# Top-32 attention with two feed-forward layers on one core: v in ten chunks of 128 rows with a column of ones, and three products per chunk into the same 65 columns

## The chip, the core and the metric

The kernel runs on one core of a Trainium2 chip. The core has five engines that work side by side, each through its own instructions in order: TensorE (PE, matrix products; its weight loads are listed apart as PEld), VectorE (DVE), ScalarE (ACT), GpSimd (POOL) and SyncE (SP, which issues the transfers). They wait for each other by semaphores. PE writes its products to a small memory of its own, PSUM, in eight banks; the rest lies in SBUF. The metric is the time of one execution on the device, in microseconds (us), as the median of several runs.

## What is computed

Four batches of eight heads with 576 positions of 64 values each. Every row of the scores keeps its 32 largest entries, the softmax runs over those, and the result goes through two feed-forward layers of 512 x 2048 x 512.

```python
scores = scale * np.matmul(q, k.transpose(0, 1, 3, 2))
kth = np.partition(scores, -top_k, axis=-1)[..., -top_k:-top_k + 1]
scores = np.where(scores >= kth, scores, -1000000000.0)
attn = np.exp(scores - np.max(scores, axis=-1, keepdims=True))
attn = attn / (np.sum(attn, axis=-1, keepdims=True) + 1e-09)
attn_out = np.matmul(attn, v)
x = attn_out.transpose(0, 2, 1, 3).reshape(B * S, H * D)
h = x @ moe_w_in;   x = np.maximum(0.01 * h, h) @ moe_w_out
h = x @ moe2_w_in;  out = (h * (1.0 / (1.0 + np.exp(-h)))) @ moe2_w_out
```

## The kernel before

**Numbers in two halves.** Every fp32 operand of a product is kept as a sum of two fp16 numbers, hi and lo, after a scaling by a power of two. A product is then hi times hi, hi times lo and lo times hi, added up in PSUM. The power of two comes from a sum of squares: ACT squares a tile and adds up each row (`kvsq`, L606), PE sums over the rows with a matrix of ones (`sum`, L550), and three small DVE steps make the factor.

**Blocks and pairs.** The 2304 positions are 18 blocks of 128 rows. Sixteen blocks lie in one batch. Two *mixed* blocks (numbers 4 and 13, from zero) hold the last 64 positions of two batches, the one in rows 0 to 63 and the other in rows 64 to 127. A block has four *pairs* of heads, so there are 72 pairs, 64 pure and 8 mixed; pair 12 below is the thirteenth. For each pair:

- `S` (L748): PE multiplies q and k into 2 x 576 scores; ACT copies them to SBUF (L760).
- `chain`: fourteen DVE steps, MAX8 and MATCH_REPLACE8 by turns (L774 to L778), find the 32nd largest of each row.
- `cut` and `exp` (ACT, L800 and L809): what is below the cut goes to zero in the exponential. `exp` also sums the row (`accum_out`, a separate ACCUMULATOR read), into `rs`.
- `p_hi` (ACT, L824) and `p_lo` (POOL, L832) make the halves of the probabilities, and a transfer transposes them into `pT`, 18 chunks of 128 positions by 128 rows.
- `pv` (PE, L862): for each of the two heads and each batch of the block ten products. The 1152 positions of two heads lie in nine chunks of v, `[128, 9, 2, D]`: four full ones for each head, and a middle one, number 4, of which each head has 64 rows. For a full chunk p_hi is multiplied with v_hi and v_lo side by side (128 columns) and p_lo with v_hi (64 columns). For the middle one both contract 64 rows only.

After two pairs (half a block) DVE makes the reciprocals from `rs` (`norm`, L878 and L884), ACT copies the v_lo columns out of PSUM (`comb_a`, L897), DVE adds the others (`comb_b`, L902), and POOL multiplies by the reciprocals (`comb_c`, L909) into `xf`.

**Feed-forward.** Per block and layer there are four steps of twelve matmuls of 512 columns into `h` (L986; from `xT` in the first layer and `yT` in the second), the activation and split on ACT, DVE (L1004, second layer only) and POOL (L1020), a transposing transfer, and four steps of twelve matmuls into `acc` (L1039). That is 16 steps of twelve matmuls per block, 288 in all.

**Weights.** In the first quarter of the span the four weight matrices are loaded as int64 words, rebuilt as fp32 by ACT and DVE (L438, L475), squared on PE (L492) for their scale, and split into halves by ACT, POOL and DVE (L527 is DVE's share of the splits).

**What sets the order.** A planner (`Plan.run`) works out the order of all engines ahead of time. Every step has an engine, a duration that is written into the code (`pv`: 1.3 us per batch), what it reads and writes, and the buffers that it takes (`BUFS`: one tile for `S`, `pv`, `acc` and `hlk`, two for `h`, three for `g`, five for `v`). By these costs and two tables of delays and preferences (`LATE`, `BOOST`) it always picks the step that can begin first, and each engine then gets its instructions in that fixed order. A changed cost can therefore move any step.

**Where v's buffers bind.** v has five tiles and a batch needs four. At a mixed block, the second batch's v tiles take the tiles of the first batch, one by one, as their last `pv` is done. The conversion `kvhi` (L632) takes the tile, so it waits for that `pv`; the square, the sum and the scaling run ahead of it.

Of the kernel before, what the change touches and what calls it, by code (L numbers as in the profile page):

```python
# [279 lines left out]
def topk_attention_moe_moe2_kernel(  # L280
# [34 lines left out]
    junk = wp.tile([128, 9 * D], BF16, name="junk")  # L315
# [265 lines left out]
    def kv_ops(which, src, b, p):  # L581
# [29 lines left out]
        add("ACT", act_t(576) + 0.1, square, r=[rk], w=[("kvss", which, b, p)], name="kvsq" + tail)  # L611
# [16 lines left out]
        def hi():  # L628
            tile_of(dk, "hlk" if which == "k" else "v", [128, 9, 2, D], F16)
# [5 lines left out]
            new=[("hlk", dk), ("k", ("k", b, p))] if which == "k" else [("v", dk)], name="kvhi" + tail, seq="kvhi")  # L635
# [95 lines left out]
    def pair_ops(s):  # L731
# [51 lines left out]
        for h in range(2):  # L783
# [345 lines left out]
```

## Time and profile before

| what | value |
| --- | --- |
| median of 3 runs | 1118.65 us (1118.25 to 1121.33) |
| span of the profiled execution | 1120.1 us, its own time on the page |
| PE, busy | 987.2 us (88%) |
| DVE, busy | 898.8 us (80%) |
| ACT, busy | 845.0 us (75%) |
| POOL, busy | 650.5 us (58%) |
| `pv` on PE (L862), 1600 matmuls, busy | 112.6 us |
| both feed-forward layers on PE (L986, L1039), busy | 797.5 us |

Busy times of an engine are the union of its instructions. Matmuls are pipelined: one is listed with some 0.2 to 0.4 us, from its start to its modelled end, and the next begins long before that. The time that a group of matmuls costs PE is therefore read from its first start to the first start of the next group.

### The profile page before, as it was taken

How to read it: one execution, taken by the hardware profiler on the slowest of the kernel's cores; microseconds unless marked ns; L12 is line 12 of the kernel's file. 1: busy time of each engine (PE TensorE's matmuls, PEld its weight loads, DVE VectorE, ACT ScalarE, POOL GpSimd, SP SyncE). 2: the span in 40 equal slices, each digit the busy share in tenths (PEclk: the TensorE clock that was granted, in tenths of full speed). 3: DMA queues.
4: the chain of work that ended last, by engine and by line, in shares of the span. 5: the costliest groups of instructions: out<-in, count | busy, mean ns of one | idle time of the engine just before them, and what ended most of it. 6: DMA issues, size and time to landing. Idle time of an engine off the chain costs nothing.

```text
span 1120.1 us, 18054 instructions
## 1 busy us (share of the span) xinstructions
PE 987.2 (88%) x6024; PEld 494.9 (44%) x6024; DVE 898.8 (80%) x1853; ACT 845.0 (75%) x1415; POOL 650.5 (58%) x885
## 2 busy tenths in 40 slices
PE   2443664879999999999999999999999999999998
PEld 1222323344444544444444544445555444444443
DVE  5999878999948999999999999974999999720000
ACT  5999998989767888887897888774888786742322
POOL 1355664869565776666786676664576655542321
PEclk9655676989999999999999999999999999999999
DMA  7995876635876687675987885776567675653432
GB/s 221 313 312 156 229 212 186 145 76 105 155 145 109 120 163 132 122 137 111 182 159 134 147 146 114 131 134 135 105 132 130 123 122 97 117 101 70 69 70 57
DMA packets 458110, 157.44 MB, mean 141 GB/s; under 512 B 440864, under 2 KB 449056, under 8 KB 455968
## 3 DMA queue, kind: packets, MB, share of 16 engines
q1 hardware_dynamic: 458016, 156.29, 67.1%
q8 instruction: 47, 0.77, 0.3%
q14 instruction: 47, 0.39, 0.1%
HBM read 47.71 MB, written 4.72 MB: 47 GB/s over the span
## 4 chain that ended last, share of the span: by engine, by line
PE 46%; DVE 26%; ACT 11%; issue 6%; POOL 6%; DMA 4%; SPq 1%; ACTq 0%; POOLq 0%; DVEq 0%
PE acc L1039 19%; PE h L986 18%; DVE w L776 9%; DVE m L778 8%; PE pv L862 4%; PE S L748 3%; DVE w_all L475 2%; DVE m L774 2%; POOL ph L832 2%; DMA pT<-ph 2%; ACT sb L809 2%; ACT sb L800 1%; PE acc L492 1%; ACT ph L824 1%; DVE w_all L527 1%
## 5 line engine op out<-in xcount | busy, mean ns | idle before, releaser
L1039 PE MATMUL acc<-w_all,gT 128*128 128x512 f16 x1728 | 400.1, 382 | 15.9 <-POOL w_all L532 5.0
L778 DVE MAX8 m<-w 128x8 f32<-128x576 f32 x432 | 307.9, 746 | 0.0
L1020 POOL TENSOR_TENSOR hl<-g,hl 128x512 f16<-128x512 f32 x144 | 173.6, 1206 | 164.2 <-ACT hl L1013 157.6
L1039 PEld LDWEIGHTS <-gT 128*128 128x128 f16 x1728 | 166.1, 99 | 213.5 <-issue 19.8
L832 POOL TENSOR_TENSOR ph<-sb,ph 128x1152 f16<-128x1152 f32 x72 | 171.1, 2376 | 114.6 <-ACT ph L824 104.8
L986 PE MATMUL h<-w_all,xT 128*128 128x512 f16 x864 | 201.4, 385 | 16.5 <-DMA xT<-hlx 15.8
L776 DVE MATCH_REPLACE8 w<-m,w 128x576 f32<-128x576 f32 x288 | 211.9, 742 | 0.0
L986 PE MATMUL h<-w_all,yT 128*128 128x512 f16 x864 | 196.0, 379 | 1.7 <-DVE g L1004 1.7
L986 PEld LDWEIGHTS <-xT 128*128 128x128 f16 x864 | 84.3, 99 | 118.0 <-DMA xT<-hlx 16.7
L809 ACT ACTIVATE sb<-sb,nb,u 128x576 f32<-128x576 f32 x144 | 124.1, 862 | 16.0 <-POOL nb L788 10.7
L986 PEld LDWEIGHTS <-yT 128*128 128x128 f16 x864 | 83.8, 98 | 100.3 <-issue 2.3
L862 PE MATMUL pv<-v,pT 128*128 128x128 f16 (+3 forms) x1600 | 112.6, 214 | 14.6 <-DMA pT<-ph 14.6
L800 ACT ACTIVATE sb<-sb,m 128x576 f32<-128x576 f32 x144 | 108.5, 766 | 21.2 <-DVE m L778 20.9
L1004 DVE SCALAR_TENSOR_TENSOR g<-g,h 128x512 f32<-128x512 f32 x72 | 48.9, 680 | 93.5 <-ACT g L999 91.0
L774 DVE MAX8 m<-sb 128x8 f32<-128x576 f32 x144 | 101.9, 745 | 11.0 <-ACT sb L760 11.0
L862 PEld LDWEIGHTS <-pT 128*128 128x128 f16 (+3 forms) x1600 | 87.4, 103 | 52.2 <-DMA pT<-ph 16.8
L760 ACT ACTIVATE sb<-S 128x1152 f32<-128x1152 f32 x72 | 81.0, 1125 | 37.6 <-POOL ph L832 30.7
L748 PE MATMUL S<-k,qT 128*128 128x64 f16 (+3 forms) x640 | 90.1, 301 | 19.3 <-DMA qT<-hlx 9.3
L1013 ACT ACTIVATE hl<-g 128x512 f16<-128x512 f32 x144 | 89.9, 625 | 21.7 <-DVE g L1004 18.1
L776 DVE MATCH_REPLACE8 w<-m,sb 128x576 f32<-128x576 f32 x144 | 105.9, 742 | 0.0
L788 POOL TENSOR_SCALAR nb<-m,u 128x1 f32<-128x1 f32 x144 | 67.7, 473 | 53.2 <-DVE m L778 50.5
L824 ACT ACTIVATE ph<-sb 128x1152 f16<-128x1152 f32 x72 | 83.5, 1159 | 5.0 <-DMA pT<-ph 3.7
(96 smaller groups left out, 1024.1 us busy)
## 6 DMA issues: line engine op xcount, KB each, us to landing
w_all<-in_moe_w_in_dram SPq DMA_DIRECT2D x16, 1024.0 KB, 5.8
w_all<-in_moe_w_out_dram SPq DMA_DIRECT2D x14, 1024.0 KB, 6.0
raw<-in_k_dram SPq DMA_DIRECT2D x16, 256.0 KB, 3.1
rawq<-in_q_dram SPq DMA_DIRECT2D x32, 128.0 KB, 2.8
raw<-in_v_dram SPq DMA_DIRECT2D x16, 256.0 KB, 3.0
out_dram<-of SPq DMA_DIRECT2D x16, 256.0 KB, 2.4
gT<-hl SPq DMA_TRANSPOSE x144, 3.2
of<-in_moe_w_out_dram SPq DMA_DIRECT2D x8, 256.0 KB, 3.1
```

What stands on the lines that cost most here:

```text
L748: nc.tensor.matmul(out=t[p0:p1, o:o + k1 - k0], lhsT=lhs, rhs=kt[:, k0:k1], start=(x == 0), stop=(x == 1),)
L774: nc.vector.max(m[:, 0], T[sbk][:, h])
L776: nc.vector.match_replace(w, m[:, step // 2], T[sbk][:, h] if step == 1 else w, NEG)
L778: nc.vector.max(m[:, step // 2], w)
L800: nc.scalar.activation(out=x, in_=x, func=AF.Prelu, scale=-1.0, bias=T["m", s][:, h, 3, 7:8], alpha=2.0**-CUT)
L809: nc.scalar.activation(out=x, in_=x, func=AF.Exp, scale=T["u", blk, hf][:, 1, p % 2:p % 2 + 1], bias=T["nb", s][:, h:h + 1], accum_out=T[" ...
L824: nc.scalar.activation(out=T[phk][:, 0, x0 * S:x1 * S], in_=T[sbk][:, x0:x1].rearrange("p h k -> p (h k)"), func=AF.Copy)
L832: nc.gpsimd.tensor_tensor(out=T[phk][:, 1, x0 * S:x1 * S], in0=T[sbk][:, x0:x1].rearrange("p h k -> p (h k)"), in1=T[phk][:, 0, x0 * S:x1 ...
L862: nc.tensor.matmul(out=o[p0:p1, h, p % 2, 0:n], lhsT=l, rhs=r, start=(i == 0), stop=(i == len(mm) - 1))
L986: nc.tensor.matmul(out=t, lhsT=a[:, ai], rhs=w_rhs(layer, wi, kk, i), start=(n == 0), stop=(n == 3 * KDM - 1))
L1020: nc.gpsimd.tensor_tensor(out=n[:, 1], in0=T[gk], in1=n[:, 0], op=ALU.subtract)
L1039: nc.tensor.matmul(out=t, lhsT=g[:, ai], rhs=w_rhs2(layer, wi, 4 * i + j), start=(i == 0 and j == 0 and n == 0), stop=(i == NCH - 1 and j ...
```

## The change

- **v** becomes `[128, 10, 129]`: 64 columns hi, one column of ones, 64 columns lo. The middle chunk stands there twice, once for each head, with zeros in the rows of the other. Four POOL instructions per v tile (`vtail`) write the ones, the copy and the zeros.
- **pv**: for each of five chunks per head, p_hi and p_lo are multiplied with v_hi and the ones (65 columns), and p_hi with v_lo (64 columns), all into the same 65 columns, always over 128 rows. That is 15 instead of 10 matmuls per head and batch, 2400 instead of 1600. In a mixed block the loop over the batches is the inner one. The planner's cost goes from 1.3 us per batch to 0.87 us, and 1.02 us for a mixed pair.
- **Row sums and combining**: the 65th column is the row sum, so `exp` no longer sums. `norm` reads the sum from PSUM, and one DVE step (`comb`) multiplies the 64 columns by the reciprocals into `xf`; `comb_a` on ACT and `comb_c` on POOL are gone. The tile in PSUM takes one bank instead of two.
- **Squares**: `kvsq` writes its squares into the v tile (or the k tile `hlk`) that it takes for that, before, not at, the conversion. The other squares go to a tile `junk` in the freed PSUM bank.
- The scaled copy of the second layer's input takes a tile of `of` instead of one of `g`.

```diff
+    VW = 2 * D + 1
-    junk = wp.tile([128, 9 * D], BF16, name="junk")
+    junk = ps.tile([128, 512], F32, name="junk", tag="junk", bufs=1)
...
         def square():
             T["kvss", which, b, p] = st_tile(1, f"kvss{which}", 4)
+            tile_of(dk, "hlk" if which == "k" else "v", [128, 9, 2, D] if which == "k" else [128, 10, VW], F16)
             nc.scalar.activation(
-                out=junk[:, 0:9 * D], in_=T[rk].rearrange("p c d -> p (c d)"), func=AF.Square,
-                accum_out=T["kvss", which, b, p],
+                out=dst(0).bitcast(BF16), in_=T[rk], func=AF.Square, accum_out=T["kvss", which, b, p],
             )
...
+        if which == "v":
+            def tails():
+                t = T[dk]
+                nc.gpsimd.memset(t[:, 0:9, D:D + 1], 1.0)
+                nc.gpsimd.tensor_copy(t[ST:128, 9, :], t[ST:128, 4, :])
+                nc.gpsimd.memset(t[0:ST, 9, :], 0.0)
+                nc.gpsimd.memset(t[ST:128, 4, :], 0.0)
+
+            add("POOL", 1.0, tails, w=[dk], name="vtail" + tail)
...
-                    bias=T["nb", s][:, h:h + 1], accum_out=T["rs", blk][:, c:c + 1],
+                    bias=T["nb", s][:, h:h + 1],
...
-                tile_of(pvk, "pv", [128, 2, 4, 128], F32)
+                tile_of(pvk, "pv", [128, 2, 2, D + 1], F32)
...
+                o = T[pvk][:, p % 2, h]
+                mm = []
+                for c, vc in [(5 * h + c, 5 * h + c) for c in range(4)] + [(4, 9 if h else 4)]:
+                    mm += [(c, vc, 0, D + 1), (9 + c, vc, 0, D + 1), (c, vc, D + 1, VW)]
+                for i, (c, vc, d0, d1) in enumerate(mm):
+                    for p0, p1, b, _ in blocks[blk]:
                         nc.tensor.matmul(
-                            out=o[p0:p1, h, p % 2, 0:n], lhsT=l, rhs=r, start=(i == 0), stop=(i == len(mm) - 1)
+                            out=o[p0:p1, 0:d1 - d0], lhsT=pT[:, c, p0:p1], rhs=T["v", b, p][:, vc, d0:d1],
+                            start=(i == 0), stop=(i == len(mm) - 1),
                         )
-        add("PE", 1.3 * len(bs), pv, r=[pTk] + [("v", b, p) for b in bs], w=[pvk],
+        add("PE", 0.87 + 0.15 * (len(bs) - 1), pv, r=[pTk] + [("v", b, p) for b in bs], w=[pvk],
...
-                    in0=T["rs", blk][p0:p1, 4 * hf:4 * hf + 4].rearrange("p (j h) -> p j h", h=2), scalar=1e-9,
+                    in0=T[pvk][p0:p1, :, :, D], scalar=1e-9,
...
+            nc.vector.tensor_tensor(
+                out=T[xk][:, 256 * hf:256 * hf + 256].rearrange("p (j h d) -> p j h d", h=2, d=D), in0=T[pvk][:, :, :, 0:D],
+                in1=T["rec", blk, hf].rearrange("p (j h o) -> p j h o", h=2, o=1).to_broadcast([128, 2, 2, D]), op=ALU.mult,
+            )
...
-                t = tile_of(yk, "g", [128, DM], F32)
+                t = tile_of(yk, "of", [128, DM], F32)
```

**On PE, the start of one pair's pv.** Before, after the sum for a v tile, each weight load of a chunk of `pT` is followed by a matmul of 128 or of 64 columns:

```order
L550 MATMUL h<-kvssv,ones 128x1
L862 LDWEIGHTS pT
L862 MATMUL pv<-v,pT 128x128
L862 LDWEIGHTS pT
L862 MATMUL pv<-v,pT 128x64
```

In the changed kernel, at the start of the same pair's pv (behind the squares of a weight matrix):

```order
L493 MATMUL acc<-w_all 128x128
L866 LDWEIGHTS pT
L866 MATMUL pv<-v,pT 128x65
L866 LDWEIGHTS pT
L866 MATMUL pv<-v,pT 128x65
L866 LDWEIGHTS pT
L866 MATMUL pv<-v,pT 128x64
```

A chunk has three narrow products where it had a wide and a narrow one.

**On DVE, at pair 12 of the attention.** Before, between the MAX and MATCH_REPLACE steps of pair 12 (`m_2041`), stand a split of the last weight matrix (L527) and gating steps of the second layer (L1004):

```order
L776 MATCH_REPLACE w<-m_2041,w 128x576 x2
L1004 SCALAR_TENSOR_TENSOR g<-g,h 128x512
L778 MAX m_2041<-w 128x8 x2
L527 SCALAR_TENSOR_TENSOR w_all<-w_all,ws_2035 128x1024
L1004 SCALAR_TENSOR_TENSOR g<-g,h 128x512
```

In the changed kernel pair 12 runs without a step of another kind, and among those of pair 13 (`m_2153`) stand the trace of the last weight matrix (L503), its scale (`ws_2261`), the two steps of `norm` and the new `comb` (L898), and the first split (L528):

```order
L503 SCALAR_TENSOR_TENSOR junk,wtot<-acc,ident 128x128
L788 MAX m_2153<-w 128x8
L883 SCALAR_TENSOR_TENSOR den<-pv,sv_75 128x4
L889 RECIPROCAL rec<-den 128x4
L356 TENSOR_SCALAR fx<-h 128x1
L357 TENSOR_SCALAR ws_2261<-fx 128x1
L358 TENSOR_SCALAR ws_2261<-fx 128x1
L898 TENSOR_TENSOR xf<-pv,rec 128x256
L786 MATCH_REPLACE w<-m_2153,w 128x576 x2
L528 SCALAR_TENSOR_TENSOR w_all<-w_all,ws_2261 128x1024
```

The splits of the last weight matrix have moved behind a later pair, and with them the layer steps that need it.

**On ACT, behind the first pv of mixed block 4.** Before, the conversion of v (L632) waits for PE, with the conversion of k and the first layer's square behind it:

```order
L824 ACTIVATE ph<-sb 128x1152
L685 ACTIVATE rawq<-rawq,qs 128x256
L632 ACTIVATE v<-raw 128x9x64
L632 ACTIVATE hlk<-raw,sk_72 128x9x64
L924 ACTIVATE junk,xss<-acc 128x512
```

In the changed kernel the square into the v tile (L608) waits there, and its scaling (L628) and conversion (L635) follow some steps later:

```order
L833 ACTIVATE ph<-sb 128x1152
L608 ACTIVATE v,kvssv<-raw 128x9x64
L991 ACTIVATE g<-h,u_2284 128x512
L930 ACTIVATE of<-acc,ys 128x512
L682 ACTIVATE junk,qss<-rawq 128x256
L1005 ACTIVATE hl<-g 128x512
```

What now begins behind that pv is the whole preparation of the v tile, not its last steps.

## Rows read from the trace of the kernel before

**Rows 1.** Page: busy us (share, instructions); busy tenths in 40 slices.

```profile
PE 987.2 (88%) x6024; PEld 494.9 (44%) x6024; DVE 898.8 (80%) x1853; ACT 845.0 (75%) x1415; POOL 650.5 (58%) x885
PE   2443664879999999999999999999999999999998
...
DVE  5999878999948999999999999974999999720000
```

**Rows 2.** Stretches: length, busy us (instructions) of each engine, PEclk, DMA share, GB/s.

```profile
0.00:100.00 100.00, 36.33 (x243) 24.26 (x244) 83.73 (x166) 81.58 (x114) 35.06 (x48) 0.70 0.91 270
100.00:200.00 100.00, 57.41 (x331) 30.84 (x330) 86.38 (x146) 90.26 (x133) 61.87 (x63) 0.65 0.67 188
...
278.25:322.70 44.45, 40.71 (x260) 19.84 (x258) 40.88 (x89) 35.68 (x64) 27.84 (x38) 0.96 0.82 147
322.70:998.46 675.76, 670.04 (x4227) 332.84 (x4227) 602.55 (x1294) 532.20 (x933) 431.95 (x623) 1.00 0.70 130
998.46:1120.10 121.64, 117.98 (x561) 53.67 (x559) 11.12 (x16) 36.40 (x60) 32.32 (x39) 1.00 0.35 68
```

**Rows 3.** PE's timeline near 600 us: start, us to the last end, instructions.

```profile
601.89 1.14 PE L748 MATMUL S<-k,qT 128*128 128x512 f16 x8
602.87 2.75 PE L986 MATMUL h<-w_all,xT 128*128 128x512 f16 x12
605.46 2.75 PE L1039 MATMUL acc<-w_all,gT 128*128 128x512 f16 x12
608.05 1.33 PE L862 MATMUL pv<-v,pT 128*128 128x128 f16 x20
609.31 2.76 PE L986 MATMUL h<-w_all,xT 128*128 128x512 f16 x12
```

**Rows 4.** A stretch inside that pv, L862 alone: length, PE, PEld busy.

```profile
608.39:608.48 0.09, 0.09 (x4) 0.01 (x1) 1.00 0.06 24
```

**Rows 5.** PE's timeline at mixed blocks: scores and the next, pv and the next.

```profile
336.20 1.20 PE L748 MATMUL S<-k,qT 128*64 128x512 f16 x16
337.33 1.47 PE L986 MATMUL h<-w_all,xT 128*128 128x512 f16 x6
...
759.81 2.73 PE L862 MATMUL pv<-v,pT 128*64 128x128 f16 x40
762.47 0.82 PE L1039 MATMUL acc<-w_all,gT 128*128 128x512 f16 x3
```

**Rows 6.** Pair 12's pv; then L986 alone and L1039 alone up to it.

```profile
278.25 1.32 PE L862 MATMUL pv<-v,pT 128*128 128x128 f16 x20
...
0.00:278.25 278.25, 47.82 (x192) 19.48 (x192) 0.75 0.73 197
...
0.00:278.25 278.25, 33.49 (x132) 12.82 (x132) 0.75 0.73 197
```

**Rows 7.** Groups by line and form: count, busy us, mean ns, idle before it.

```profile
L862 PEld LDWEIGHTS <-pT 128*128 128x128 f16 x1024 | 55.8, 103 | 34.5 <-DMA pT<-ph 16.8 <-issue 0.8
L862 PEld LDWEIGHTS <-pT 128*64 128x64 f16 x256 | 12.9, 111 | 4.6 <-issue 3.0
L527 DVE SCALAR_TENSOR_TENSOR w_all<-w_all,ws 128x1024 f16<-128x1024 f32 x15 | 20.7, 1383 | 0.0
L1004 DVE SCALAR_TENSOR_TENSOR g<-g,h 128x512 f32<-128x512 f32 x72 | 48.9, 680 | 93.5 <-ACT g L999 91.0 <-POOL hl L1020 1.9
L809 ACT ACTIVATION_READ_ACCUMULATOR sb<-sb,nb,u 128x1 f32 x144 | 27.1, 188 | 0.0
L606 ACT ACTIVATE junk<-raw 128x576 bf16<-128x576 f32 x32 | 21.5, 673 | 4.2 <-DMA raw<-in_k_dram 2.9 <-DMA raw<-in_v_dram 1.3
L643 POOL TENSOR_TENSOR v<-raw,v 128x576 f16<-128x576 f32 x12 | 15.3, 1279 | 3.4 <-ACT v L632 3.4
L356 POOL TENSOR_SCALAR xs<-fx 128x1 int32<-128x1 int32 x18 | 3.4, 190 | 1.5
```

**Rows 8.** Waits: who waited for whom, us in total, times, longest.

```profile
ACT v L632 <- PE pv L862: 4.2, 3, 2.3
```

More of the change, by code (lines that the diff above doesn't have):

```diff
@@ L605, in square @@
             T["kvss", which, b, p] = st_tile(1, f"kvss{which}", 4)
+            tile_of(dk, "hlk" if which == "k" else "v", [128, 9, 2, D] if which == "k" else [128, 10, VW], F16)
             nc.scalar.activation(
[L607 to L611 removed]
+                out=dst(0).bitcast(BF16), in_=T[rk], func=AF.Square, accum_out=T["kvss", which, b, p],
+            )
+        add("ACT", act_t(576) + 0.1, square, r=[rk], w=[dk, ("kvss", which, b, p)],
+            new=[("hlk" if which == "k" else "v", dk)], name="kvsq" + tail)
         sum_op(("kvss", which, b, p))
@@ L619, in dst @@
         def dst(x):
+            if which == "v":
+                return T[dk][:, 0:9, (D + 1) * x:(D + 1) * x + D]
             return T[dk][:, :, x, :]
@@ L634, in kv_ops @@
         add("ACT", act_t(576, 1), hi, r=[rk, sn], w=[dk],
-            new=[("hlk", dk), ("k", ("k", b, p))] if which == "k" else [("v", dk)], name="kvhi" + tail, seq="kvhi")
+            new=[("k", ("k", b, p))] if which == "k" else [], name="kvhi" + tail, seq="kvhi")
         def lo():
@@ L886, in comb_ops, with comb @@
         add("DVE", 0.16 + 0.17 * len(bs), norm,
-            r=[("rs", NP * blk + 2 * hf + j, h) for j in range(2) for h in range(2)]
-            + [("s", "v", b, 2 * hf + j) for b in bs for j in range(2)],
+            r=[pvk] + [("s", "v", b, 2 * hf + j) for b in bs for j in range(2)],
             w=[("rec", blk, hf)], name="norm" + tail)
-        def half():
-            return T[xk][:, 256 * hf:256 * hf + 256].rearrange("p (j h d) -> p j h d", h=2, d=D)
-        def comb_a():
+        def comb():
             if hf == 0:
                 tile_of(xk, "xf", [128, DM], F32)
-            nc.scalar.activation(out=half(), in_=T[pvk][:, :, 0:2, D:2 * D].rearrange("p h j d -> p j h d"), func=AF.Copy)
-        add("ACT", act_t(256), comb_a, r=[pvk], w=[(xk, hf)], new=[("xf", xk)] if hf == 0 else [], name="comb_a" + tail, seq="comb_a")
-        def comb_b():
-            nc.vector.tensor_tensor(out=half(), in0=T[pvk][:, :, 0:2, 0:D].rearrange("p h j d -> p j h d"), in1=half(), op=ALU.add)
-        add("DVE", 0.35, comb_b, r=[pvk], w=[(xk, hf)], name="comb_b" + tail)
-        def comb_c():
-            r = T["rec", blk, hf].rearrange("p (h o) -> p h o", o=1).to_broadcast([128, 4, D])
-            dst = T[xk][:, 256 * hf:256 * hf + 256].rearrange("p (h d) -> p h d", d=D)
-            nc.gpsimd.tensor_tensor(out=dst, in0=dst, in1=r, op=ALU.mult)
-        add("POOL", 0.65, comb_c, r=[("rec", blk, hf)], w=[(xk, hf)], name="comb_c" + tail)
+            nc.vector.tensor_tensor(
+                out=T[xk][:, 256 * hf:256 * hf + 256].rearrange("p (j h d) -> p j h d", h=2, d=D), in0=T[pvk][:, :, :, 0:D],
+                in1=T["rec", blk, hf].rearrange("p (j h o) -> p j h o", h=2, o=1).to_broadcast([128, 2, 2, D]), op=ALU.mult,
+            )
+        add("DVE", 0.35, comb, r=[pvk, ("rec", blk, hf)], w=[(xk, hf)], new=[("xf", xk)] if hf == 0 else [], name="comb" + tail, seq="comb")
     def split_ops(layer, blk):
```

26 lines of the change are left out of this document (6 added, 20 removed).

## The prediction

> **What bounds the kernel now.** Read the page's busy shares and slices first [rows 1]: TensorE (PE) is busy 88% of the span, VectorE (DVE) 80%, and the slices show when. In the first quarter PE has three to eight tenths and DVE eight or nine; from there on PE has nine or more in every slice, while DVE drops to seven or less in the last four. The busy time by stretches [rows 2] makes this sharp. From 322.70 to 998.46 PE is idle 5.7 us of 675.8, and in the last 121.6 us it works nearly alone (118.0 busy, DVE 11.1). So the end is the moment from which PE has work without a break, plus all the work that it then still has. Before 278.25 PE waits instead: in the first 200 us it is busy 94 us, DVE 170 and ScalarE (ACT) 172, since the weights are being split there. A microsecond saved on PE counts from about 278 on; before that, the order on DVE and ACT counts.
>
> The third view is PE's timeline [rows 3]. Call twelve matmuls of 512 columns a quantum: it takes 605.46 - 602.87 = 2.59 us, 0.216 each. Scores (S) take 0.98 us for four matmuls of 512 columns and four of 64, so a 64-column one takes (0.98 - 4 x 0.216) / 4 = 29 ns, its weight load included. A straight line through 64 and 512 columns gives 56 ns at 128 and 29.4 at 65. The product of probabilities and v (pv) of a pure pair takes 609.31 - 608.05 = 1.26 us for ten matmuls of 128 and ten of 64 columns, which by the line should take 0.85. The other 0.41 lies where the contraction changes between 128 rows and 64: four changes per pair, 0.10 each. A narrow slice inside that pv [rows 4] shows one of them: 0.09 us with 0.01 of weight loading in it.
>
> **The change, part by part.** *Pure pairs.* With every chunk on 128 rows the four changes go. Thirty matmuls remain, 20 x 29.4 + 10 x 29 = 0.88 us. That is 0.38 less per pair, and the next instruction has the same tile shape, so nothing is owed at the exit. From the thirteenth pair (number 12, at 278.25 [rows 6]) on there are 52 pure pairs: 19.8 us.
>
> *Mixed pairs.* Forty matmuls take 762.47 - 759.81 = 2.66 us [rows 5], one batch after the other. Scores of a mixed pair, on the same two column halves, take 337.33 - 336.20 = 1.13 us for twice the matmuls of a pure pair (0.98): the halves overlap. At that ratio the sixty alternating matmuls take 1.15 x 0.88 = 1.01 us; without overlap they take 1.76, with a complete one 0.88. I take 1.01, as scores are the nearest row. Eight pairs, 1.65 each: 13.2 us. Against this, the Trainium skill ("TensorEngine Tiling (Array Packing)", section "Restrictions") says that column tiling disables fast weight loading. An estimate with the load time of "TensorE: Matmul & The Clock Gate" ("LDWEIGHTS"), columns over 1.2, is 53 ns a load, 3.2 us for sixty, and 17 us worse over eight pairs. The old mixed pair contradicts it: 2.66 less eight changes of 0.10 is 46 ns per matmul with its load.
>
> *Order on DVE and PE.* New costs move everything. Before, PE has done 192 / 12 + 132 / 12 = 27 quanta when pair 12's pv starts [rows 6]; in the changed order 17 stand ahead of it, 34 against 39 at pair 16, 54 in both at pair 19. So up to ten quanta (25.9 us) of layer work leave a stretch where PE idles and enter the one where it is full. In return pair 12 can come sooner: ahead of its last chain step DVE has two weight splits of 1.38 us, two gating steps of 0.68 and small steps of about 1.1 us fewer [rows 7], 5.3 us. ACT has 26 accumulator reads of 0.188 us fewer by then, 4.9 us, which helps only where ACT is late; I count 1 us of it. Pair 12's pv so starts near 272 instead of 278.25, with 262 and 280 as the ends (all of DVE's early waiting on ACT gone, or one new wait).
>
> *ACT, DVE and POOL elsewhere.* ACT loses the accumulator reads, 27.1 us in all [rows 7], and the copies out of PSUM; POOL loses the scaling; on DVE one step of 256 columns takes the place of another. From 322 on DVE has 73 us to spare [rows 2] and PE's work covers all of it: nothing. Four small POOL steps per v tile are new, sixteen times. The smallest POOL step takes 0.19 us; the conversion of 576 columns 1.28, so 129 columns take 0.29 at its rate [rows 7]. Four cost 0.8 to 1.2 us per tile, and I take 1.2. POOL is 58% busy; they count only where a pv waits for the tile, next.
>
> *The v tile is claimed earlier.* Squaring now writes into the tile, so at mixed blocks ACT's square waits until the last pv has left a buffer; before, only the later conversion did. Behind the square on ACT stands the second layer's activation, for which DVE's gating step and then PE's next quanta wait, and the sum over the square stands on PE itself, in front of quanta. From that pv to the next pv that needs the tile lies this chain: the square 0.67 and its accumulator read 0.19, a sum on PE and three one-column steps on DVE (taken like the smallest POOL step, 4 x 0.19), two ACT steps over the same columns as the square (2 x 0.67), the conversion 1.28, the four new steps 1.2: 5.4 us [rows 7]. PE's order has at least four quanta, 10.4 us, in between, at all six places, so the cover is 5.0 us. ACT's three waits of this kind cost 4.2 us in all, on ACT [rows 8]. I take nothing; where the cover fails the price is up to 1.5 us a place, 9 us.
>
> **The sum.** From pair 12 to the end the profiled execution takes 1120.1 - 278.25 = 841.9 us. Plus 25.9, minus 19.8 and 13.2, that is 834.8. PE's 3.7 us of waiting between 278 and 322 [rows 2] should go, with ten quanta more at hand: 831. From 272 on this ends at 1103, 17 us below the span. The span is 1.5 us above the median of the three runs (1118.65, 1118.25 to 1121.33), so the forecast is 1101 us, 1.6% faster.
>
> **The rivals.** *The early delay costs nothing.* Pair 12 comes 10 us or more earlier, because ACT's relief shortens DVE's waits. For it speaks ACT's load of 90% between 100 and 200 us; against it, that DVE's work ahead of pair 12 falls by 5.3 us only. The gain on PE is then kept nearly whole: 1118.65 - 33 = 1086.
>
> *The halves do not overlap and the v chain is late.* Both sit at the mixed blocks: 8 x 0.75 = 6 us and 9 us, 1101 + 15 = 1116. Scores' 1.13 us speaks against the first, the 5.0 us of cover against the second.
>
> *Weight loads set the pace (slower).* Today a narrow matmul always stands beside a wide one, whose streaming covers a load. Thirty narrow ones in a row show whether a load fits into 29 ns. If it does not, the busy time of the loads is the nearest price: 55.8 us for 1024, 54 ns [rows 7], so 30 x 0.054 = 1.63 us for a pure pair, and 60 x 12.9 / 256 = 3.0 for a mixed one. The sum becomes 1101 + 52 x 0.75 + 8 x 2.0 = 1156 us. It decides from about 42 ns a load, where a pure pair costs its old 1.26. Against it: scores have two such matmuls in a row and still average 29 ns. The Trainium skill ("TensorE: Matmul & The Clock Gate", "Back-to-back issue gap") gives this rule: in a stream of load and matmul the spacing is set by both, 81 ns at 128 columns. By that page even the wide ones here would be slower than the 56 ns that the rows give.
>
> *The new order makes DVE the bound.* DVE now waits for pv itself before it normalises, and pairs come closer together; if its waiting eats the 73 us, the last pv stays at about 998. Then 40 quanta follow instead of 45: 1118.65 - 13 = 1106 at best, and with pair 12 late by as much, 1119, the case of no change. About 0.3%, 3.4 us, is what a measurement of this kernel can tell from none.
>
> **Chances.** The forecast, 1101 (1093 to 1109): 0.57. Early delay free, 1086: 0.16. Trouble at the mixed blocks, 1116: 0.11. Loads set the pace, 1156: 0.07. DVE or the order, 1106 to 1120: 0.09. The range that holds eight in ten is 1085 to 1116: down to pair 12 at 262 and PE's last waits gone, up to pair 12 at 280 and no overlap. Below 1115.3 lie the first two, half of the third and half of the last: faster 0.83; within 0.3% 0.08; slower 0.09.
>
> **What would show it.** On PE's timeline of the changed kernel a pure pv takes 0.88 us and a mixed one about 1.0; near 1.6 and 3.0 the loads set the pace, at 1.76 the halves do not overlap. Pair 12's pv starts near 272 us, and PE idles more than 90 us before it. After it PE idles under 10 us; 40 quanta, 104 us, follow the last pv. PE waiting for POOL ahead of a pv at a mixed block would show the late v tile. The forecast fails if pair 12 comes after 280 us, or if PE waits for DVE between 322 and the last pv.

## The result and the profile after

The changed kernel takes 1101.76 us (median of 4 runs, 1101.11 to 1102.31) where the kernel before, on the same chip, takes 1119.06 (1118.25 to 1121.33): a ratio of 0.9841, with a 95% interval of 0.9827 to 0.9855. The profiled execution spans 1100.1 us. The forecast was 1101 by a span of 1103. The time came out; two terms behind it did not, and they nearly cancel, so that it came out so closely is luck.

Page of the changed kernel: busy us (share, instructions), and PE's and DVE's busy tenths in 40 slices, to be held against [rows 1].

```profile
PE 957.0 (87%) x6824; PEld 486.4 (44%) x6824; DVE 896.0 (81%) x1853; ACT 823.2 (75%) x1235; POOL 637.4 (58%) x913
...
PE   2434735668999999999999999999999999999998
...
DVE  4999989998948999999999999994899999951010
```

PE has 800 instructions more and 987.2 - 957.0 = 30.2 us less to do. The picture is that of before: PE waits in the first quarter and is full behind it, and DVE drops off in the last slices.

Stretches of the changed kernel, cut where [rows 2] were cut: at pair 12's pv (259.44), at pair 16's (311.81) and at the last pair's (991.71). Columns: length, busy us (instructions) of PE, PEld, DVE, ACT and POOL, granted clock, DMA share, GB/s.

```profile
259.44:311.81 52.37, 52.37 (x361) 26.14 (x359) 47.96 (x98) 42.29 (x64) 36.39 (x37) 0.96 0.68 122
311.81:991.71 679.90, 670.27 (x4980) 335.88 (x4980) 605.30 (x1303) 529.86 (x820) 432.98 (x652) 1.00 0.73 133
991.71:1100.10 108.39, 104.70 (x511) 47.78 (x509) 10.08 (x16) 32.19 (x53) 27.46 (x35) 1.00 0.38 66
```

The 3.7 us that PE waited just behind pair 12 are gone (52.37 of 52.37 busy). From there to the last pv it now waits 679.90 - 670.27 = 9.6 us, where [rows 2] have 3.7 and 5.7. The tail has lost five quanta: 104.70 us of PE against 117.98.

PE's timeline of the changed kernel: start, us to the last end, instructions, and in brackets idle time before them with what ended it. The time of a group is from its start to the start of the next one.

```profile
257.57 2.08 PE L760 MATMUL S<-k,qT 128*128 128x512 f16 x8 [5.19 <-ACT sb L772]
259.44 1.85 PE L866 MATMUL pv<-v,pT 128*128 128x65 f16 x30
...
604.57 1.11 PE L866 MATMUL pv<-v,pT 128*128 128x65 f16 x30
605.52 0.81 PE L1031 MATMUL acc<-w_all,gT 128*128 128x512 f16 x3
...
754.21 1.15 PE L866 MATMUL pv<-v,pT 128*64 128x65 f16 x60
755.29 1.47 PE L978 MATMUL h<-w_all,xT 128*128 128x512 f16 x6
```

A pure pv now takes 605.52 - 604.57 = 0.95 us (before 1.26, [rows 3]) and a mixed one 755.29 - 754.21 = 1.08 (before 2.66, [rows 5]). Pair 12's pv starts at 259.44, not at 278.25 [rows 6].

Both kernels up to pair 12's pv and from there to the last pv: first the kernel before, then the changed one, same columns.

```profile
0.00:278.25 278.25, 158.46 (x981) 88.53 (x982) 244.30 (x455) 240.68 (x360) 158.35 (x188) 0.75 0.73 197
278.25:998.46 720.21, 710.75 (x4485) 352.68 (x4484) 643.43 (x1383) 567.89 (x997) 459.80 (x660) 1.00 0.71 131
```

```profile
0.00:259.44 259.44, 129.70 (x979) 76.64 (x980) 232.64 (x437) 218.84 (x300) 140.55 (x190) 0.75 0.77 206
259.44:991.71 732.27, 722.64 (x5338) 362.02 (x5337) 653.26 (x1401) 572.14 (x883) 469.37 (x689) 0.99 0.73 132
```

So 18.8 us are won ahead of pair 12, although PE waits more there (129.7 us after 119.8), and only 1.2 us behind it: 1100.1 - 259.4 = 840.7 against 841.9. Nearly all that the faster pv gives behind pair 12 is taken up by the ten quanta that were moved there.

### The profile page after: what moved, and what is told of

It reads as the page before. It is cut to its first block, busy times and chain, and to the rows that moved or that the text cites. A ratio compares the mean times of both kernels' runs of the same rounds, so it can differ in the third digit from the quotient of the medians.

```text
span 1100.1 us, 19543 instructions
## 1 busy us (share of the span) xinstructions
PE 957.0 (87%) x6824; PEld 486.4 (44%) x6824; DVE 896.0 (81%) x1853; ACT 823.2 (75%) x1235; POOL 637.4 (58%) x913
## 4 chain that ended last, share of the span: by engine, by line
PE 49%; DVE 20%; ACT 11%; issue 7%; POOL 6%; DMA 5%; SPq 1%; ACTq 0%; POOLq 0%; DVEq 0%
PE acc L1031 21%; PE h L978 20%; DVE w L786 7%; DVE m L788 6%; PE S L760 3%; PE pv L866 3%; POOL ph L841 2%; DMA pT<-ph 2%; ACT sb L818 2%; DVE w_all L476 2%; DVE m L784 1%; ACT sb L810 1%; POOL hl L1012 1%; ACT w_all L439 1%; PE acc L493 1%
## 5 line engine op out<-in xcount | busy, mean ns | idle before, releaser
L760 PE MATMUL S<-k,qT 128*128 128x64 f16 (+3 forms) x640 | 94.2, 309 | 51.7 <-ACT sb L772 28.9
L772 ACT ACTIVATE sb<-S 128x1152 f32<-128x1152 f32 x72 | 81.0, 1125 | 46.5 <-POOL ph L841 44.7
L866 PEld LDWEIGHTS <-pT 128*128 128x128 f16 (+1 forms) x2400 | 81.4, 104 | 29.1 <-DMA pT<-ph 13.7
L866 PE MATMUL pv<-v,pT 128*128 128x65 f16 (+3 forms) x2400 | 85.3, 199 | 9.4 <-DMA pT<-ph 9.3
L798 POOL TENSOR_SCALAR nb<-m,u 128x1 f32<-128x1 f32 x144 | 63.6, 445 | 49.3 <-DVE m L788 46.7
L760 PEld LDWEIGHTS <-qT 128*128 128x128 f16 (+1 forms) x640 | 44.5, 106 | 100.8 <-issue 45.6
```

Of the source, the lines that this page charges most:

```text
L760: nc.tensor.matmul(out=t[p0:p1, o:o + k1 - k0], lhsT=lhs, rhs=kt[:, k0:k1], start=(x == 0), stop=(x == 1),)
L866: nc.tensor.matmul(out=o[p0:p1, 0:d1 - d0], lhsT=pT[:, c, p0:p1], rhs=T["v", b, p][:, vc, d0:d1], start=(i == 0), stop=(i == len(mm) - 1),)
```

## Experiments

The theory to be tested is the prediction's: PE is the bound, its work shrinks by what the changes of tile shape and the missing overlap cost, and the planner's new order puts enough quanta in front of the last pv to use that. The main rivals left: DVE is the bound in the changed kernel; pair 12 came early because ACT was relieved; the order's part is small. Each ratio is to the kernel before on the same chip. The numbers of quanta are counted in the order of PE's instructions.

### The two halves of the change apart: the cost and the product

**e1_old_cost** is the changed kernel with the old number in the planner.

```diff
-        add("PE", 0.87 + 0.15 * (len(bs) - 1), pv, r=[pTk] + [("v", b, p) for b in bs], w=[pvk],
+        add("PE", 1.3 * len(bs), pv, r=[pTk] + [("v", b, p) for b in bs], w=[pvk],
```

> The changed kernel with one number put back: the planner's cost of pv is 1.3 us per batch again, so the instructions are the same and only the order differs (17 quanta ahead of pair 12 as in the changed kernel, but 242 instead of 248 ahead of the last pv). Theory A, PE's work adds up: pair 12's pv near 259 us as in the changed kernel, PE full after it, span 1100 to 1104; the last pv comes some 15 us earlier, near 976. Theory B, DVE sets when the last pv comes: last pv near 990, 46 quanta behind it, span 1115.

**e2_new_cost_old_pv** is the kernel before with the new number.

```diff
-        add("PE", 1.3 * len(bs), pv, r=[pTk] + [("v", b, p) for b in bs], w=[pvk],
+        add("PE", 0.87 + 0.15 * (len(bs) - 1), pv, r=[pTk] + [("v", b, p) for b in bs], w=[pvk],
```

> The kernel before with only the planner's cost of pv changed to 0.87 us (1.02 for a mixed pair); all instructions are the old ones, the order has 248 instead of 243 quanta ahead of the last pv and 25 instead of 27 ahead of pair 12. Theory A: PE has the same work and two quanta more of it behind pair 12, so 1119 to 1125 us, no gain. Theory B, the gain is the order's: last pv near 996, 40 quanta behind it, 1106.

| | planned at 1.3 us per batch | planned at 0.87 us (mixed 1.02) |
| --- | --- | --- |
| old pv | 1119.06 us (the kernel before; 1120.64 beside e1 and e2) | 1129.30 (1128.87 to 1130.16), ratio 1.0086 [1.0069, 1.0103] |
| new pv | 1125.27 (1123.98 to 1126.22), ratio 1.0048 [1.0034, 1.0063] | 1101.76, ratio 0.9841 [0.9827, 0.9855] |

Stretches of e1 (cut at pair 12's and the last pv), columns as above:

```profile
0.00:260.30 260.30, 132.15 (x979) 78.49 (x980) 232.66 (x437) 218.80 (x300) 142.23 (x190) 0.74 0.75 205
260.30:999.40 739.10, 713.50 (x5267) 356.68 (x5266) 651.30 (x1399) 568.14 (x873) 461.36 (x680) 0.99 0.71 130
999.40:1123.30 123.90, 120.20 (x583) 54.81 (x581) 11.44 (x18) 37.95 (x63) 34.20 (x44) 1.00 0.37 66
```

PE's waits in the middle stretch of e1: who waited for whom, us in total, times, longest.

```profile
PE S L760 <- ACT sb L772: 8.0, 14, 1.9
PE acc L1031 <- ACT of L1044: 4.6, 2, 4.1
PE pv L866 <- DMA pT<-ph: 3.0, 3, 1.7
```

The same of the changed kernel:

```profile
PE S L760 <- ACT sb L772: 3.6, 4, 2.2
PE acc L1031 <- DMA gT<-hl: 2.2, 4, 1.0
PE acc L1031 <- ACT of L1044: 1.5, 2, 1.4
```

With the old cost, the fast pv is worth nothing. Pair 12 comes at 260.3 as in the changed kernel, but 242 quanta instead of 248 stand ahead of the last pv. PE waits 739.1 - 713.5 = 25.6 us on the way to it, and 46 quanta follow. Neither theory of the expectation gave this time (1100 to 1104, or 1115). The reading that the planner takes PE for busy where it is not, and so leaves quanta for later, fits the list of waits, but no run shows it by itself.

Stretches of e2, cut in the same way:

```profile
0.00:280.50 280.50, 154.60 (x956) 86.38 (x957) 248.22 (x458) 240.32 (x355) 150.58 (x179) 0.85 0.73 195
280.50:1016.70 736.20, 727.11 (x4569) 361.54 (x4568) 646.91 (x1382) 574.08 (x1008) 464.81 (x672) 1.00 0.71 130
1016.70:1127.70 111.00, 105.23 (x501) 47.78 (x499) 9.42 (x14) 30.92 (x53) 27.95 (x36) 1.00 0.32 65
```

In e2, 248 quanta stand ahead of the last pv, as in the changed kernel; PE is full (9.1 us idle in 736) and simply has more to do, so the last pv comes at 1016.7. The sum of the prediction fits here: two quanta fewer than before stand ahead of pair 12, so 280.5 + 841.85 + 2 x 2.59 = 1127.5, and the span is 1127.7; the expected 1119 to 1125 lacked the later pair 12. Neither half of the change gains anything alone. Both together do. The new number is also not what moved ten quanta behind pair 12: e1 has 17 ahead of it with the old number, e2 has 25 with the new one. That shift comes with the other changes to the steps; what the number moves is six quanta (242 to 248) to the front of the last pv.

### The products themselves

**e3_halves_apart** takes the alternation of the two batches out of mixed pairs. The order of all other instructions stays.

```diff
-                for i, (c, vc, d0, d1) in enumerate(mm):
-                    for p0, p1, b, _ in blocks[blk]:
+                for p0, p1, b, _ in blocks[blk]:
+                    for i, (c, vc, d0, d1) in enumerate(mm):
```

> The changed kernel with the loop over the batches of a mixed pair put outside again: fifteen matmuls of one batch, then fifteen of the other, for each head; order of everything else unchanged. Theory A with overlap only by alternating: a mixed pv takes about 1.9 us instead of 1.08, eight of them, 1101.8 + 7 = 1109. If the halves overlap in any order, as for the scores: no change, 1102. Theory B: PE's extra time is covered, 1102 to 1104.

Measured: 1105.47 us (1103.84 to 1107.23), ratio 0.9873 [0.9853, 0.9892], span 1105.1. PE's timeline of e3 at the mixed pair that stood at 754.21:

```profile
756.97 1.81 PE L866 MATMUL pv<-v,pT 128*64 128x65 f16 x60
758.71 2.55 PE L978 MATMUL h<-w_all,xT 128*128 128x512 f16 x11
```

A mixed pair takes 1.74 us instead of 1.08, which is 60 products of 29 ns one after the other. Eight times 0.66 is 5.3 us; the profiled span has grown by 5.0 and the median by 3.7. The halves overlap when they alternate, and not in two rows of fifteen.

**e4_middle_64_rows** brings the 64-row contraction back for the middle chunk. The second head then multiplies the 64 rows of zeros in its copy of the chunk, so its middle positions are left out; the number of products is that of the changed kernel.

```diff
+                        r1 = ST if c in (4, 13) else 128
...
-                            out=o[p0:p1, 0:d1 - d0], lhsT=pT[:, c, p0:p1], rhs=T["v", b, p][:, vc, d0:d1],
+                            out=o[p0:p1, 0:d1 - d0], lhsT=pT[0:r1, c, p0:p1], rhs=T["v", b, p][0:r1, vc, d0:d1],
```

> The changed kernel with the three products of each middle chunk contracted over 64 rows only (both heads over rows 0 to 63, so the second head's middle positions are wrong); same number of matmuls, same order, but four changes of tile shape per pair are back. Theory A: a pure pv takes 0.95 + 0.40 = 1.35 us, 52 of them after pair 12 and 8 mixed: 22 to 25 us longer, 1125. Theory B: PE's extra time is covered by DVE's, under 8 us longer.

Measured: 1117.90 us (1116.41 to 1120.70), ratio 0.9981 [0.9971, 0.9991], span 1114.6. PE's timeline of e4 at a pure and at a mixed pair:

```profile
608.70 1.41 PE L867 MATMUL pv<-v,pT 128*128 128x65 f16 x30
610.04 1.25 PE L1032 MATMUL acc<-w_all,gT 128*128 128x512 f16 x5
...
761.26 1.50 PE L867 MATMUL pv<-v,pT 128*64 128x65 f16 x60
762.69 0.60 PE L979 MATMUL h<-w_all,xT 128*128 128x512 f16 x2
```

A pure pair takes 1.34 us instead of 0.95: four changes of the contraction, 0.10 each, as [rows 4] had shown. Mixed pairs go from 1.08 to 1.43. From pair 12 on that is 52 x 0.39 + 8 x 0.35 = 23.1 us. PE's busy time grows by 24.1 (981.2 after 957.0), its idle time falls by 9.7 (143.1 to 133.4), and the span grows by the difference, 14.5, where 22 to 25 had been expected. So the full chunks are worth 14 to 16 us, most of the gain, and e4 stands almost where the kernel before stood.

### What is late ahead of pair 12, and what bounds the kernel behind it

**e5_exp_sums** gives ACT its row sums back (144 accumulator reads; the sums go to a column that nobody reads), in the same order.

```diff
-                    bias=T["nb", s][:, h:h + 1],
+                    bias=T["nb", s][:, h:h + 1], accum_out=T["m", s][:, h, 1, 0:1],
```

> The changed kernel with the row sums put back into the exponential (written to a spare column and not used): ACT gets its 144 accumulator reads of 0.19 us back, 27 us, 26 of them ahead of pair 12; the order of all engines is the same. If ACT's relief is what brought pair 12's pv to 259 us, 13 us sooner than predicted: pair 12 at 266 to 275 us and the end 1108 to 1115. If it is the order (DVE's work ahead of pair 12) alone: pair 12 at 259 to 263, 1102 to 1105.

Measured: 1107.75 us (1107.72 to 1108.03), ratio 0.9888 [0.9873, 0.9902]. Stretches of e5:

```profile
0.00:261.10 261.10, 130.61 (x979) 76.22 (x980) 232.50 (x436) 220.50 (x325) 140.27 (x189) 0.74 0.75 205
261.10:997.50 736.40, 724.66 (x5337) 362.16 (x5336) 654.69 (x1401) 583.06 (x1003) 470.06 (x691) 0.99 0.73 132
```

Pair 12 comes 1.7 us later, not 18.8: the accumulator reads that ACT lost are not what brought it forward. (The copies out of PSUM that ACT lost as well, and DVE's waits for the sums, stay away in e5; no run brings them back.) Behind it the sums cost 4.1 us (736.4 after 732.3), half of it as PE's waiting, and the end lies above the 1102 to 1105 that was expected with an early pair 12. So the removal of the sums is worth some 6 us in all (5 by the ratios).

**e8_six_of_seven** leaves out the third MATCH_REPLACE step of every chain, so that the row is cut at another entry. That takes 1.5 us per pair, 107 us in all, off DVE.

```diff
+                elif step == 5:
+                    pass
```

> The changed kernel without the third MATCH_REPLACE8 step of every chain (so the cut is at another entry): DVE has 1.5 us less per pair, 107 us in all; order unchanged. If PE's work decides from pair 12 on: pair 12's pv comes 10 to 19 us sooner, PE's 9.6 us of idle time behind it shrink to 3 to 5, and the end is 1076 to 1088. If DVE's chains set when the last pv comes: the last pv moves by far more than that, by 50 us or more, with PE idle no longer than now, and the end is below 1060.

Measured: 1093.95 us (1093.78 to 1094.24), ratio 0.9765 [0.9748, 0.9781]. Stretches of e8:

```profile
0.00:255.60 255.60, 130.57 (x978) 77.85 (x979) 215.18 (x381) 218.80 (x300) 140.85 (x190) 0.73 0.78 209
255.60:983.60 728.00, 720.00 (x5338) 361.81 (x5337) 572.53 (x1169) 570.95 (x883) 470.00 (x690) 1.00 0.73 133
```

DVE does 98 us less by its busy time (797.8 after 896.0 in all), and the end comes 8 us sooner: 3.8 ahead of pair 12, 4.3 behind it. Between pair 12 and the last pv the freed time turns into idle time of DVE, and PE stays at 99%. Both expectations missed: pair 12 was to come 10 to 19 us sooner and PE's 9.6 us of idle time behind it to shrink to 3 to 5 (it is 8.0), or else the end was to fall below 1060. The last pv moved by 8.1 us and not by 50, so behind pair 12 PE is the bound in this order, not DVE.

### How much hangs on the order

Seven kernels with the same 6824 instructions on PE, the same products and different orders. **e7_cost_095** names the cost that the trace gives; **e9_cost_080** and **e10_cost_105** lie at either side of it. **c1_tables** and **c2_tables** keep the cost of e7 and change some numbers in the planner's tables of preferences and delays so that 24 quanta stand ahead of pair 12.

```diff
-        add("PE", 0.87 + 0.15 * (len(bs) - 1), pv, r=[pTk] + [("v", b, p) for b in bs], w=[pvk],
+        add("PE", 0.95 + 0.13 * (len(bs) - 1), pv, r=[pTk] + [("v", b, p) for b in bs], w=[pvk],
```

> The changed kernel with the planner's cost of pv at the durations that the trace shows, 0.95 us and 1.08 for a mixed pair; instructions unchanged, the order has 20 quanta ahead of pair 12 (17 before) and 245 ahead of the last pv (248). PE's sum: the same work and no new idle time, 1099 to 1104. If the number of quanta that the order leaves behind the last pv decides, with the last pv at 992 as before: three more, 1102 + 8 = 1110.

e9 has `0.80 + 0.15 * (len(bs) - 1)` there:

> The changed kernel, planner's cost of pv 0.80 us (0.95 mixed) in place of 0.87 (1.02); another order of the same instructions, with 17 quanta ahead of pair 12 and 248 ahead of the last pv as in the changed kernel. If the gain depends on the number of quanta that the order puts ahead of the last pv: 1100 to 1104. If the order of the changed kernel was a lucky one among many: 1106 or more, as with 0.95 (1108.2).

e10 has `1.05 + 0.13 * (len(bs) - 1)`:

> The changed kernel, planner's cost of pv 1.05 us (1.18 mixed); the order has 22 quanta ahead of pair 12 and 244 ahead of the last pv. Between the old cost (242 ahead, 1125.3) and 0.95 (245 ahead, 1108.2): 1108 to 1116 if the quanta ahead of the last pv decide; PE's sum alone (pair 12 near 265, five quanta fewer left behind it than in the changed kernel) would give 1094.

c1 is e7 with these lines ahead of the planner:

```diff
+for _k, _v in {'s_copy': 200, 'sum': 100, 'kvsc': 30, 'bias': -60, 'of': 100, 'ylo': -100, 'p_lo': -100,
+               'wjoin3': -60, 'gtr': -30, 'ghi': -30, 'kvhi': -100, 'yhi': -60, 'wlo3': -60, 'ysq': -30, 'norm': -60}.items():
+    BOOST[_k] = BOOST.get(_k, 0) + _v
+for _k, _v in {'S': 2, 'kvsc': 0.8, 'o0': 0.2, 'kvsq': 0.5, 'kvhi': 1.2, 'norm': 2, 'cut': 1.2, 'kvlo': 0.2,
+               'qload': 1.2, 'qsc': 1.2, 'ptr': 0.8}.items():
+    LATE[_k] = LATE.get(_k, 0) * _v
```

> The changed kernel with the planner's cost of pv at 0.95 and 1.08 us and other numbers in the two tables of preferences and delays; same instructions, with 24 quanta ahead of pair 12 (17 in the changed kernel) and 247 ahead of the last pv (248). PE's sum: pair 12's pv near 264 and seven quanta (18 us) fewer behind it: 264 + 840.7 - 18.1 = 1086, 1082 to 1094. If the last pv stays at 992 and the quanta behind it decide: 1104.

c2 is e7 with others:

```diff
+for _k, _v in {'whi2': 30, 'xsq': -30, 'wlo2': 60, 'kvsc': 200, 'ptr': -60, 'comb': 200, 'wjoin3': -30,
+               'kvhi': 60, 'ylo': -60, 'of': -60, 'cut': 60, 'p_hi': 30, 'kvscale': -30}.items():
+    BOOST[_k] = BOOST.get(_k, 0) + _v
+for _k, _v in {'cut': 0.8, 'h0': 1.2, 'kvlo': 0.2, 'S': 0.5, 'kvload': 0.8, 'kvhi': 0.5, 'o1': 1.2, 'store': 2}.items():
+    LATE[_k] = LATE.get(_k, 0) * _v
```

> As the one before with another set of numbers in the tables: 24 quanta ahead of pair 12 and 251 ahead of the last pv. PE's sum: 1082 to 1094. If the last pv stays at 992 and the quanta behind it decide (37): 1094.

| kernel | cost, pure / mixed | quanta ahead of pair 12 / of the last pv | pair 12, us | A | B | A + B | span | median, us (range) | ratio [95%] |
| --- | --- | --- | --- | --- | --- | --- | --- | --- | --- |
| e1 | 1.30 / 2.60 | 17 / 242 | 260.3 | 216.3 | 29.3 | 245.6 | 1123.3 | 1125.27 (1123.98 to 1126.22) | 1.0048 [1.0034, 1.0063] |
| e10 | 1.05 / 1.18 | 22 / 244 | 265.2 | 208.2 | 28.4 | 236.6 | 1112.2 | 1114.08 (1111.32 to 1114.88) | 0.9943 [0.9924, 0.9962] |
| e7 | 0.95 / 1.08 | 20 / 245 | 263.6 | 211.8 | 23.0 | 234.8 | 1108.7 | 1108.23 (1107.64 to 1110.49) | 0.9895 [0.9880, 0.9910] |
| changed | 0.87 / 1.02 | 17 / 248 | 259.4 | 215.4 | 13.3 | 228.7 | 1100.1 | 1101.76 (1101.11 to 1102.31) | 0.9841 [0.9827, 0.9855] |
| e9 | 0.80 / 0.95 | 17 / 248 | 259.5 | 215.5 | 14.8 | 230.3 | 1098.6 | 1101.34 (1100.35 to 1104.14) | 0.9842 [0.9820, 0.9864] |
| c1 | 0.95 / 1.08 | 24 / 247 | 263.6 | 201.4 | 19.4 | 220.8 | 1091.3 | 1094.64 (1093.12 to 1096.39) | 0.9774 [0.9757, 0.9792] |
| c2 | 0.95 / 1.08 | 24 / 251 | 268.0 | 205.8 | 9.9 | 215.7 | 1082.9 | 1084.40 (1083.12 to 1086.51) | 0.9684 [0.9666, 0.9702] |

A is the start of pair 12's pv less 2.59 us for each quantum that PE has done by then, B is PE's idle time from there to the end. Of the expectations, those of e9, e10 and c2 came in; e7 (1108.23) lies 2 us short of "the quanta left behind the last pv decide", and c1 (1094.64) between its two, because the last pv does not stay at 992: it comes between 980 (c1) and 999.4 (e1). The order alone is worth 41 us, more than twice what the change gained. With the same tables, the cost nearest to the truth does not give the best order: with 0.95 the end is 6 us later than with 0.87, and 0.80 is as good as 0.87. A + B falls as the spans do (the changed kernel and e9 are level), by 29.9 of the 40.4 us between e1 and c2; the other 10.5 it leaves open. Neither the moment of pair 12 alone nor the waits alone would sort them. c2 is the fastest with pair 12 latest, because it has done seven quanta more than the changed kernel by then and waits least afterwards.

Stretches of e10 and then of c2, the two ends of it apart from e1:

```profile
0.00:265.20 265.20, 149.85 (x1038) 86.65 (x1039) 234.01 (x441) 227.63 (x311) 150.13 (x190) 0.73 0.75 202
265.20:991.20 726.00, 703.40 (x5229) 351.45 (x5228) 648.16 (x1396) 561.16 (x867) 457.04 (x688) 0.99 0.73 132
991.20:1112.20 121.00, 115.22 (x559) 52.40 (x557) 10.37 (x17) 33.69 (x57) 30.77 (x37) 1.00 0.35 66
```

```profile
0.00:268.00 268.00, 144.85 (x1063) 82.12 (x1064) 239.58 (x446) 230.36 (x316) 147.81 (x192) 0.80 0.76 202
268.00:982.30 714.30, 708.07 (x5291) 355.92 (x5290) 640.78 (x1393) 559.42 (x870) 459.34 (x689) 1.00 0.74 136
982.30:1082.90 100.60, 96.89 (x475) 44.15 (x473) 10.15 (x16) 30.28 (x50) 26.15 (x33) 0.99 0.36 66
```

Added up, PE is busy 968.5 us in e10 and 949.8 in c2, and idle 143.7 and 133.1. Of the 29.3 us between the two spans, idle time is 10.6 and busy time 18.7, with the same instructions. Ahead of pair 12, c2 does 25 more of them in 5.0 us less, at a granted clock of 0.80 where e10 has 0.73. Whether the order brought the higher clock is not shown: the four runs of e10 had mean clocks of 0.929 to 0.960 (spans 1109.4 to 1113.0) and those of c2 0.943 to 0.956 (1081.2 to 1084.6), so the clock differs between runs of one order as much as between the two traces. Which entry of c2's tables brings its gain was not separated, and no run gives the kernel before other tables, so how much of that gain needs the new pv stays open.

Against the changed kernel, c2's last pv comes 9.4 us sooner and three quanta fewer follow it (7.8 us): 17.2, the whole difference of the spans. **c2 beats both kernels**, with 1084.40 us.

## Why the prediction was right, and where it was not

**What bounds the kernel: right.** PE is full from pair 12 to the last pv (722.64 of 732.27 us), and e8 shows that relieving DVE by a tenth brings under one per cent. What the other parts of the change bring by themselves (one `comb` step, the places of the squares, the tile of `of`) no run shows.

**The pv of a pair: right in kind, a little short in size.** The changes of shape cost 0.10 each (e4), and they are gone. But a pure pair takes 0.945 us, not 0.88: in a stream of narrow products each costs 31.5 ns instead of the 29.4 that the straight line from scores gave. A mixed pair takes 1.08, not 1.01; the overlap is there (e3), and the ratio taken from scores holds (1.08 / 0.945 = 1.14, where 1.15 was said), so its miss is that of the pure pair over again. From pair 12 on that is 52 x 0.065 + 8 x 0.07 = 3.9 us less gained.

**The ten quanta behind pair 12: right.** 17 stand ahead of it, 40 follow the last pv, and the tail has 104.70 us of PE work where 104 was said.

**Pair 12 at 272: this step failed.** It came at 259.44, outside of the 262 to 280 that I gave. Up to the end of pair 12's chain, and from there to its pv, first the kernel before, then the changed one (the stretch up to the chain's end, the chain's last steps, the cut of the second head, `p_lo`, the issue of the transfer):

```profile
0.00:255.49 255.49, 137.08 (x860) 78.34 (x860) 224.16 (x419) 220.08 (x325) 137.09 (x164) 0.73 0.74 203
254.08 1.41 DVE L778 MAX8 m<-w 128x8 f32<-128x576 f32 x2
260.15 0.77 ACT L800 ACTIVATE sb<-sb,m 128x576 f32<-128x576 f32 x1
268.03 2.37 POOL L832 TENSOR_TENSOR ph<-sb,ph 128x1152 f16<-128x1152 f32 x1
270.43 2.69 SPq L841 DMA_TRANSPOSE pT<-ph  x1
```

```profile
0.00:243.40 243.40, 118.85 (x862) 68.49 (x863) 218.70 (x406) 204.51 (x282) 128.97 (x170) 0.75 0.78 213
241.99 1.41 DVE L788 MAX8 m<-w 128x8 f32<-128x576 f32 x2
244.67 0.76 ACT L810 ACTIVATE sb<-sb,m 128x576 f32<-128x576 f32 x1
247.67 2.38 POOL L841 TENSOR_TENSOR ph<-sb,ph 128x1152 f16<-128x1152 f32 x1 [3.46 <-ACT ph L833]
250.08 2.74 SPq L850 DMA_TRANSPOSE pT<-ph  x1
```

The chain ends 12.1 us sooner (243.40 after 255.49). DVE's work ahead of that is 5.5 us less, as forecast with 5.3; but DVE also waits 6.6 us less there, of which I had counted 1. In the kernel before, 2.8 of these waits were for `exp`'s sums (L878) and 1.6 for ACT's copy out of PSUM (L897), and both steps now take what they need from PSUM themselves (who waited for whom ahead of 255.49, as above; neither pair stands in the changed kernel's list):

```profile
DVE den L878 <- ACT sb L809: 2.8, 2, 1.6
DVE xf L902 <- ACT xf L897: 1.6, 1, 1.6
```

From the chain's end to the issue of the transfer it takes 6.7 us instead of 14.9, and this I had put at nothing: before, ACT does steps of the second layer, a copy of scores and weight splits between the cuts and exponentials of pair 12; in the changed kernel it does pair 12's steps one after the other. The rest goes the other way: the transfer lands after 4.7 us (4.6 before), and the pv then waits 4.7 us for its turn on PE (3.2 before), behind scores that wait for ACT's copy (the line at 257.57 above). Together that is 5.5 + 6.6 + 8.3 - 0.1 - 1.4, the 18.8 us.

In the seven kernels with 17 quanta ahead (changed, e1, e3, e4, e5, e8, e9) the way from the chain's end to the transfer takes 6.7 to 8.5 us, and pair 12 comes between 255.6 and 261.1; with 20 to 27 ahead it takes 8.8 to 21.5, and pair 12 comes between 263.6 and 280.5. That fits with ACT having fewer layer steps in its queue, but it is a comparison over whole orders and not one cause isolated. What e5 does isolate is the accumulator reads: 1.7 us, close to the 1 us that I had counted.

**From pair 12 to the end, 831: also failed, the other way.** It took 840.7. Of the 9.7 us, 3.9 are the dearer pv above. PE's waiting did not shrink by 3.7 us; it went from behind pair 12 to new places (9.6 us against 9.5 before), among them 2.20 us for ACT's copy of the scores at 552 and 1.35 for ACT's copy out of `acc` at 421. The granted clock is 0.99 in that stretch instead of 1.00, which may be the other 2 us; I have no run that isolates them. The two misses, 12.6 us too late and 9.7 too short, leave the span 2.9 us below the forecast; that they cancel is luck.

**ACT, DVE and POOL elsewhere at nothing: wrong for ACT.** The sums alone are worth 4.1 us behind pair 12 (e5), half of it through PE's waits. "DVE has 73 us to spare" was a poor reading as well. Its idle time lies in a few places, as at the mixed blocks, and from 500 to 700 it is busy 95%. It did no harm here only because PE is fuller still. Groups of the changed kernel, the last two for the next paragraph (count, busy us, mean ns, idle before them):

```profile
L883 DVE SCALAR_TENSOR_TENSOR den<-pv,sv 64x4 f32<-64x4 f32 x8 | 1.2, 156 | 7.9 <-PE pv L866 7.8
L653 POOL COPY v<-v 64x129 f16<-64x129 f16 x16 | 4.6, 290 | 10.1 <-DVE v L642 9.3
L608 ACT ACTIVATE v<-raw 128x576 bf16<-128x576 f32 x16 | 10.8, 676 | 5.6 <-DMA raw<-in_v_dram 5.0 <-PE pv L866 0.5
```

**The v tile claimed earlier, at nothing: right.** ACT's square waits 0.5 us in all for PE's pv, where the conversion waited 4.2 [rows 8], and no pv waits for POOL or for v. A later claim was not tried. Four POOL steps per tile take (2.3 + 4.6 + 3.2 + 3.2) / 16 = 0.83 us, within the 0.8 to 1.2 given.

**The rivals.** *Early delay free*: pair 12 did come more than 10 us sooner, not through ACT's accumulator reads (e5) but, by the rows above, in good part through ACT's other steps, which no run isolates; the gain on PE was not kept whole. *Halves and the v chain*: e3 and the row above exclude both. *DVE as the bound*: e8 excludes it; the order itself, which I had put into the same rival with a small chance, is by far the larger matter (1084 to 1125 us). *Weight loads set the pace*: thirty narrow products in a row run at 31.5 ns each with their loads. The rule in the Trainium skill ("TensorE: Matmul & The Clock Gate", "Back-to-back issue gap") gives 81 ns at 128 columns. The changed kernel's pv has no such products; the wide ones of the kernel before took about 57 ns, (1.26 - 0.40 - 0.29) / 10, an estimate from [rows 3], e4 and scores, and the measurement decides against the rule here. The Trainium skill ("TensorEngine Tiling (Array Packing)", "Restrictions") also says that column tiling disables fast weight loading. The alternating mixed pair has sixty products and sixty loads in 1.08 us, 18 ns a piece, so the measurement decides against the 53 ns a load that the prediction estimated from it; whether fast loading is off there no run shows.

## What to carry to other kernels

On an engine that is the bound, a cheaper step is worth something only as far as the order brings other work forward into the freed time, so the instructions and the plan have to be changed, and costed, together: here either of them alone was a loss. Where a planner's costs set a fixed order, treat them as knobs to be measured and not as truths; among four costs with the same tables the truest was not the best, and the order that paid most (c2) has the truest cost with other tables, and its pair 12 comes later than in any other order of the new products. When a step moves in time, follow it through the queue of every engine between its first input and its start, and read spare time of an engine by stretches, not as a sum.

## What the hardware showed that I had not expected

- Products of 65 columns, each with a weight load of its own, follow each other at 31.5 ns on average (0.945 us for thirty), 2.5 ns slower than the estimate of 29 ns from scores, where narrow ones stand beside wide ones.
- Two column halves that alternate cost 1.08 us for sixty products and sixty loads; the same in rows of fifteen on one half cost 1.74 (e3). In the records of the pair at 754.21 the starts of two halves lie 2 to 5 ns apart.
- A change of tile shape on PE costs about 0.1 us: four of them, between 128 and 64 rows of contraction, cost 0.39 (e4). In e4's records one start follows another by 0.12 to 0.13 us at each of these, both ways, where it is 0.03 elsewhere; at the end of a mixed pair it is 0.13 too.
- The same instructions on PE took 949.8 us of busy time in the trace of c2 and 968.5 in that of e10, at a mean granted clock of 0.950 and 0.929. How much of this is the order's stays open, since e10's own runs go from 0.929 to 0.960.
